# A new order of all pieces in a fused attention and maxout kernel, with w3 loaded first

## The chip, the cores and the metric

The kernel runs on one core of one Trainium2 chip. The metric is the device time of one execution in microseconds (us); lower is better. Engines are called by their names in the profile: PE is TensorE (matrix products; PEld is its weight load), DVE is VectorE, ACT is ScalarE, POOL is GpSimd, SP is SyncE.

## The reference

Eight batches, eight heads, 576 positions, head size 64, 32 memory slots. An attention through 32 slots feeds a maxout layer:

```
a      = softmax(phi, axis = positions)            # 8 x 8 x 576 x 32
k_m    = a^T k ;  v_m = a^T v                      # per head: 32 x 64
attn   = softmax(q k_m^T / 8, axis = slots)        # 576 x 32
x      = attn v_m, heads side by side              # 4608 x 512
h      = max(x w1, x w2, x w3)                     # 4608 x 768
out    = h w_out                                   # 4608 x 512
```

Inputs and output are fp32; the kernel computes in bf16 with fp32 accumulation.

## The kernel before, in words

The kernel does not form x. It multiplies the small v_m into the weights ("fold") and uses attn directly. It also takes w3 out of the maximum: max(x w1, x w2, x w3) is x w3 + max(0, x (w1 - w3), x (w2 - w3)), so the third product needs no maximum and goes through w3 w_out, which is made once (w3T, w3o).

The whole kernel is cut into pieces, and a list at its end (lines 594 to 619) gives their order by hand: a letter, a number and a batch, as F6@1, is one call of `issue`. Each engine takes its instructions in the order in which the list issues them, so the list is the order of every engine at once. An exclamation mark hands the eviction of that piece from ACT to DVE or the other way (`EVAC`, line 164, has the rule without the mark). A string of digits (lines 138 to 146) gives each piece its banks of PSUM, of which there are eight; a piece waits until the eviction of the piece that had its bank is done.

The pieces, with the lines at which the profile shows them:

- L0 to L3: loads of phi, k, v and q of a batch, through POOL's queue (lines 93, 97, 110); phi of batch 0 goes through SP (line 91) ahead of the list. H: a half of k (H0, H2) or v (H1, H3) of batch 0, by pairs of heads. Y0 to Y2: loads of w1, w2, w3 (line 116); Y3: w_out (line 123). All of POOL's loads stand in one queue in the order of the list.
- Z: warm-up matmuls on zeros (line 159), whose results nobody reads. I: the identity and ones, on POOL.
- E: exp(phi) on ACT (line 229). B: a^T k and a^T v, 72 small matmuls (line 249); for batches 0 and 1 B0 does k and B1 does v, for the others B does both, out of a packed copy that r0 and r1 make on POOL (line 103, 2.1 us each). N: the division by the sum on DVE (lines 269, 273, 283). K: the transpose on PE (line 298) and its eviction; K@0 also makes the negative kvtn on ACT (line 304).
- Q0, Q1: transposes of q on DVE (line 313), each waiting for q's load. S: the scores, 32 small matmuls (line 333), then two exps on ACT (line 342).
- For batch 0: M (sums by a matmul, line 354), R (1/sum as exp(-ln) on ACT, lines 366, 372), X (the product on DVE, line 377). For the others: a, s, c on DVE (lines 387, 395, 404), m on POOL (line 409), X on DVE (line 417).
- W, O: w3T and w3o on PE (lines 184, 192), evicted by DVE and by ACT. V: w1 - w3 and w2 - w3 in place, on DVE (line 213). D0 to D2: the folded weights of a batch, 512 columns each (line 440; for batch 0 D0, D1, D2 and D4, with w3 subtracted by further matmuls through kvtn); D3: the folded w3o.
- F0 to F11: the maxout products of a batch, four matmuls each (line 466). Even numbers are w1 - w3, evicted with relu into h (lines 170, 174); odd ones are w2 - w3, whose maximum with h DVE writes to hT (line 479).
- T0 to T4: 128 rows of the output: six matmuls hT by w_out (line 497) and two of attn by the folded w3o (line 506). T4 has 64 rows of each of two batches, so its four matmuls with the folded w3o are narrow, 128 by 64 (line 515). The eviction (line 172 or 176) is followed by the store through SP (line 527). T3@7 is the last piece and goes in two halves (lines 538, 546, 555 to 559).

B, D, S and T4's four use a part of PE's array per matmul ("narrow"); the others use all of it ("wide").

Of the kernel before, what the change touches and what calls it, by code (L numbers as in the profile page):

```python
# [15 lines left out]
def kernel(  # L16
# [18 lines left out]
    NG = NP // 2  # L35
    HP = P // 2
# [4 lines left out]
    FT = DF // P  # L41
# [91 lines left out]
    for i in range(P // M):  # L133
# [14 lines left out]
    def one_bank():  # L148
        return psum[:, int(next(banks))]
# [16 lines left out]
    def evacuate(kind, n, swap, out_, in_, relu=False):  # L166

        if (EVAC[kind][n] == "a") != swap:
            if relu:
                nc.scalar.activation(out=out_, in_=in_, func=AF.Relu)  # L170
            else:
                nc.scalar.copy(out=out_, in_=in_)  # L172
        elif relu:
            nc.vector.tensor_scalar_max(out=out_, in0=in_, scalar1=0.0)
        else:
            nc.vector.tensor_copy(out=out_, in_=in_)
# [245 lines left out]
    wps, wp3s = {}, {}  # L422
# [65 lines left out]
    def ffn2(b, t, swap):  # L488


        hT, attn = hts[b // 2], attns[b // 2]
        c0 = S - HP if t == 4 else (b % 2) * (S + HP) + t * P
        if b == B - 1 and t == 3:
            return ffn2_last(b, c0)
        po = one_bank()
        for n, fc in enumerate(fts[b]):
            nc.tensor.matmul(  # L497
                po,
                lhsT=hT[:, fc, c0 : c0 + P],
                rhs=wo_sb[:, fc, :],  # L500
                start=(n == 0),
                stop=False,
            )
        for g in range(NG):
            if t < 4:
                nc.tensor.matmul(  # L506
                    po,
                    lhsT=attn[:, g, c0 : c0 + P],
                    rhs=wp3s[b][:, g, :],
                    start=False,  # L510
                    stop=(g == NG - 1),
                )
            else:
                for u in range(2):
                    nc.tensor.matmul(  # L515
                        po[HP * u : HP * (u + 1)],
                        lhsT=attn[:, g, c0 + HP * u : c0 + HP * (u + 1)],
                        rhs=wp3s[b - 1 + u][:, g, :],
                        start=False,
                        stop=(g == NG - 1),  # L520
                        tile_position=(0, HP * u),
                    )
        ot = opool.tile([P, DM], FP32, name="ot")
        r0 = (b // 2) * 2 * S + c0
        rows = out[r0 : r0 + P, :]
        evacuate("T", t, swap, ot, po)
        nc.sync.dma_start(out=rows, in_=ot)

    def ffn2_last(b, c0):

        hT, attn = hts[b // 2], attns[b // 2]
        ot = opool.tile([P, DM], FP32, name="ot")
        r0 = (b // 2) * 2 * S + c0
        for i in range(2):
            c = slice(i * DM // 2, (i + 1) * DM // 2)
            po = one_bank()[:, 0 : DM // 2]
            for n, fc in enumerate(fts[b]):
                nc.tensor.matmul(  # L538
                    po,
                    lhsT=hT[:, fc, c0 : c0 + P],  # L540
                    rhs=wo_sb[:, fc, c],
                    start=(n == 0),
                    stop=False,
                )
            for g in range(NG):
                nc.tensor.matmul(  # L546
                    po,
                    lhsT=attn[:, g, c0 : c0 + P],
                    rhs=wp3s[b][:, g, c],
                    start=False,  # L550
                    stop=(g == NG - 1),
                )
# [39 lines left out]


    for w in """
        E@0 L1@0 L3@0 Z25@0 B0@0 I@0 N0@0 Z2@0 K0@0! Q0@0 Q1@0 Z9@0 S@0 Z2@0 M0@0 M1@0
        R0@0 Y2@0 R1@0 W0@0 Y3@0 W1@0 W2@0 Z6@0 O1@0 H3@0 O3@0 O2@0 H1@0 X1@0 B1@0 X0@0 N1@0
        K1@0 O0@0 Y0@0 D1@0! D0@0! D3@0 F8@0 F10@0 F2@0 V0@0 F6@0 F0@0! Y1@0 D2@0 D4@0 F4@0
        L0@1 V1@0 F1@0 E@1 F3@0 L1@1 F5@0 F9@0 F7@0 L3@1 F11@0 B0@1 T3@0 N0@1 K0@1! L2@1 Q1@1
        L2@2 L1@2 Q0@1 L0@2 V2@0 T0@0! L3@2 S@1 T1@0 a0@1 s0@1 c0@1 m0@1 B1@1 N1@1 a1@1 L1@3
        K1@1 s1@1 D0@1 D1@1! D2@1 c1@1 m1@1 X0@1 L3@3 r1@2 X1@1 T2@0! L2@3 F6@1 F10@1 F7@1 F2@1  # L600
        F3@1 F4@1 F0@1 r0@2 E@2 F5@1 F1@1 F11@1 L0@3 L0@4 F8@1 L2@4 F9@1 B@2 D3@1 N@2 Q1@2
        T0@1! K@2 T2@1! r0@3 Q0@2 S@2 a0@2 a1@2 s1@2 c1@2 m1@2 T4@1! D1@2! s0@2 D2@2 c0@2 m0@2
        X1@2 D0@2 T3@1 Q0@3 L3@4 X0@2 Q1@3 T1@1 F0@2 F4@2 F8@2 F6@2 F9@2 E@3 F7@2 r1@3 F5@2
        F10@2 F1@2 B@3 L1@4 D3@2 N@3 L0@5 F2@2 F11@2 E@4 F3@2 L1@5 K@3 r1@4 L2@5 T2@2! S@3 T3@2
        a0@3 s0@3 c0@3 m0@3 D0@3 D2@3 a1@3 s1@3 c1@3 X0@3 D1@3! Q0@4 m1@3 T1@2 L3@5 L2@6 T0@2!
        X1@3 F10@3 r0@4 F2@3 F4@3 E@5 Q1@4 r0@5 F5@3 F3@3 L1@6 F8@3 B@4 N@4 D3@3 F9@3 F6@3
        F11@3 L0@6 K@4 F0@3 F7@3 F1@3 S@4 a0@4 T4@3! s0@4 a1@4 D0@4 c0@4 s1@4 r1@5 c1@4 D3@4
        m0@4 X0@4 Q0@5 T0@3! D1@4! D2@4 B@5 T3@3 m1@4 X1@4 L0@7 F10@4 Q1@5 N@5 F8@4 K@5 F6@4
        F9@4 S@5 F7@4 L3@6 F2@4 F4@4 a0@5 L1@7 a1@5 F0@4 s0@5 r1@6 F3@4 D0@5 r0@6 s1@5 c1@5 E@6
        D3@5 m1@5 c0@5 F1@4 T1@3 L2@7 F11@4 L3@7 E@7 F5@4 m0@5 B@6 D1@5! D2@5 X1@5 N@6 T2@3!  # L610
        X0@5 F6@5 F8@5 Q0@6 Q1@6 K@6 F4@5 F9@5 S@6 F7@5 r0@7 a0@6 F2@5 a1@6 s0@6 c0@6 F0@5
        F10@5 m0@6 F1@5 s1@6 c1@6 F11@5 F5@5 T0@4! F3@5 X0@6 T2@4! r1@7 D0@6 D1@6! Q0@7 B@7
        m1@6 N@7 X1@6 T2@5! K@7 T3@4 Q1@7 S@7 a0@7 F2@6 s0@7 a1@7 s1@7 c1@7 m1@7 c0@7 F4@6
        T4@5! D3@6 D2@7 D0@7! T0@5! D3@7 D2@6 X1@7 m0@7 D1@7! T1@4 X0@7 F6@7 F3@6 T1@5 F4@7
        F8@7 F0@7 F5@6 F10@6 F7@7 F9@7 F10@7 F5@7 F0@6 F11@7 F6@6 F1@7 F7@6 F2@7 F8@6 F11@6
        F9@6 F1@6 F3@7 T0@6! T0@7! T3@5 T2@7! T2@6! T1@6 T1@7 T3@6 T4@7! T3@7
    """.split():
        n, b = w.rstrip("!").split("@")
        issue(int(b), n, w.endswith("!"))
# [30 lines left out]
```

## Time and profile before

| what | value |
|---|---|
| time, median of 3 runs (lowest to highest) | 166.47 us (166.17 to 166.52) |
| span of the profiled execution, first to last instruction | 163.9 us |
| mean granted clock of PE | 1.000 |
| PE busy | 153.8 us (94%), 2080 matmuls |
| DVE, ACT, POOL busy | 90.4, 100.5, 68.8 us |
| DMA moved | 31.77 MB, mean 194 GB/s |
| warm-up matmuls (line 159) | 44, 12.0 us |

The page gives the profiled execution by its span alone; the timed runs hold what lies around the span as well. Matmuls are pipelined: the duration of one (0.38 us for 512 columns) is longer than its distance from the next (0.2155 us), so the distance from start to start is the price of a matmul in a row of them. A bracket in the timeline names the idle time of the engine just before a group and what ended it.

### The profile page before, as it was taken

The numbers are of one execution on the slowest core, as the hardware profiler recorded it, in microseconds if no ns is written. First come the engines' busy times: TensorE is split into PE (matmuls) and PEld (weight loads), VectorE is DVE, ScalarE is ACT, GpSimd is POOL, SyncE is SP. The second block draws the span as 40 slices with busy tenths as digits, with TensorE's granted clock in tenths as the row PEclk, the third lists the DMA queues.
The fourth block names the chain that finished last, engine by engine and source line by source line (L and its number), as shares of the span: only waits on it lengthen the run. The fifth ranks groups of instructions, "written<-read, shape, count | busy, mean of one in ns | idle before, by whom it ended". The sixth has DMA issues, their size and how long they took to land.

```text
span 163.9 us, 4837 instructions
## 1 busy us (share of the span) xinstructions
PE 153.8 (94%) x2080; PEld 85.3 (52%) x2080; DVE 90.4 (55%) x181; ACT 100.5 (61%) x151; POOL 68.8 (42%) x70
## 2 busy tenths in 40 slices
PE   7958798999899999999999999999999999999990
PEld 2423544664376436753673565576553467744450
DVE  2013703898837765759399669879749228810000
ACT  4104535935496488778885989994658976323320
POOL 7911115100698276938929986755403200000000
PEclk9999999999999999999999999999999999999999
DMA  5999999999999999999999999996313230014333
GB/s 149 167 201 207 207 209 226 264 208 209 258 310 239 209 272 361 263 219 294 247 265 206 236 352 254 167 235 148 127 72 119 79 128 0 0 68 179 141 128 130
DMA packets 21958, 31.77 MB, mean 194 GB/s; under 512 B 1200, under 2 KB 16560, under 8 KB 21936
## 3 DMA queue, kind: packets, MB, share of 16 engines
q0 software_dynamic: 16064, 21.43, 68.5%
q1 hardware_dynamic: 5728, 9.90, 17.1%
q8 instruction: 16, 0.26, 0.6%
q10 hardware_dynamic: 144, 0.13, 0.2%
q14 instruction: 6, 0.05, 0.1%
HBM read 39.32 MB, written 9.44 MB: 297 GB/s over the span
## 4 chain that ended last, share of the span: by engine, by line
PE 66%; DMA 27%; POOL 3%; issue 1%; ACT 1%; ACTq 0%; POOLq 0%
PE psum L497 25%; PE psum L466 22%; DMA ph<-in_phi_dram 14%; DMA w_sb<-in_moe_w_dram 12%; PE psum L506 7%; PE psum L440 4%; PE psum L249 3%; PE psum L333 2%; PE psum L515 1%; POOL kvo L97 1%; PE psum L538 1%; ACT e L229 1%; PE psum L298 1%; POOL wo_sb L123 1%; POOL qq L110 0%
## 5 line engine op out<-in xcount | busy, mean ns | idle before, releaser
L497 PE MATMUL psum<-wo_sb,hT 128*128 128x512 bf16 x210 | 51.4, 380 | 0.2
L466 PE MATMUL psum<-attn,wp 128*128 128x288 bf16 x384 | 50.5, 286 | 0.1
L479 DVE TENSOR_TENSOR hT<-psum,h 128x576 bf16<-128x576 f32 x48 | 34.2, 749 | 18.2 <-PE psum L466 12.1
L466 PEld LDWEIGHTS <-wp 128*128 128x128 bf16 x384 | 36.7, 98 | 13.2 <-issue 2.0
L172 ACT COPY ot<-psum 128x512 f32<-128x512 f32 x35 | 20.7, 591 | 32.3 <-PE psum L506 25.2
L497 PEld LDWEIGHTS <-hT 128*128 128x128 bf16 x210 | 19.2, 98 | 24.2 <-issue 4.5
L103 POOL COPY kvr<-kvo 128x2304 bf16<-128x2304 bf16 x12 | 25.4, 2116 | 14.1 <-DMA kvo<-in_k_dram 6.4
L172 ACT CAST wp<-psum 128x1024 bf16<-128x1024 f32 (+1 forms) x31 | 29.3, 997 | 3.0 <-PE psum L440 2.1
L170 ACT ACTIVATE h<-psum 128x576 bf16<-128x576 f32 x47 | 28.4, 659 | 3.2 <-PE psum L466 3.1
L409 POOL TENSOR_TENSOR t<-t,sm 128x576 bf16<-128x576 bf16 x14 | 16.1, 1158 | 25.6 <-DVE sm L404 25.5
L506 PE MATMUL psum<-wp,attn 128*128 128x512 bf16 x62 | 18.4, 379 | 0.0
L159 PE MATMUL psum<-warm 128*128 128x512 bf16 x44 | 12.0, 424 | 1.2 <-DVE warm L128 1.2
L313 DVE STREAM_TRANSPOSE qT<-qq 128x576 f32<-128x576 f32 x16 | 11.7, 747 | 1.3 <-DMA qq<-in_q_dram 1.3
L342 ACT ACTIVATE e<-psum 128x576 bf16<-128x576 f32 x16 | 9.6, 652 | 3.7 <-PE psum L333 3.7
L229 ACT ACTIVATE e<-ph 128x1152 bf16<-128x1152 f32 (+1 forms) x9 | 9.6, 1065 | 2.9 <-DMA ph<-in_phi_dram 2.9
L395 DVE TENSOR_REDUCE sm<-t 128x18 f32<-128x576 bf16 x14 | 10.3, 738 | 0.2
L387 DVE STREAM_TRANSPOSE t<-e 128x288 f32<-128x288 f32 x14 | 6.4, 465 | 6.2 <-ACT e L342 6.0
L506 PEld LDWEIGHTS <-attn 128*128 128x128 bf16 x62 | 6.1, 98 | 7.1
L97 POOL DMA_DIRECT2D kvo<-in_v_dram x9 | 6.7, 747 | 7.1 <-PE psum L249 4.1
L249 PEld LDWEIGHTS <-e 64*32 64x32 bf16 x720 | 6.9, 90 | 4.9 <-issue 3.6
L555 DVE COPY ot<-psum 128x256 f32<-128x256 f32 x1 | 0.4, 425 | 15.4 <-PE psum L546 15.4
L110 POOL DMA_DIRECT2D qq<-in_q_dram x8 | 6.2, 769 | 5.9 <-DMA w_sb<-in_moe_w_dram 5.9
(57 smaller groups left out, 113.8 us busy)
## 6 DMA issues: line engine op xcount, KB each, us to landing
out_dram<-ot SPq DMA_DIRECT2D x35, 256.0 KB, 5.6
kvo<-in_k_dram POOLq DMA_DIRECT2D x8, 576.0 KB, 13.3
qq<-in_q_dram POOLq DMA_DIRECT2D x8, 576.0 KB, 12.6
ph<-in_phi_dram POOLq DMA_DIRECT2D x7, 576.0 KB, 15.0
kvo<-in_v_dram POOLq DMA_DIRECT2D x7, 576.0 KB, 16.6
w_sb<-in_moe_w_dram POOLq DMA_DIRECT2D x3, 768.0 KB, 20.3
wo_sb<-in_moe_w_out_dram POOLq DMA_DIRECT2D x1, 768.0 KB, 15.9
ph<-in_phi_dram SPq DMA_DIRECT2D x2, 288.0 KB, 3.1
```

What stands on the lines that cost most here:

```text
L103: nc.gpsimd.tensor_copy(out=kvrs[b % 2][:, :, :, D * i : D * (i + 1)], in_=kvos[b % 2][:, 1 - i])
L159: nc.tensor.matmul(po[:, 0:BANK], lhsT=warm[:, 0:P], rhs=warm, start=True, stop=True)
L170: nc.scalar.activation(out=out_, in_=in_, func=AF.Relu)
L172: nc.scalar.copy(out=out_, in_=in_)
L229: nc.scalar.activation(out=s["e"][:, js], in_=loaded[b]["ph"][:, js], func=AF.Exp)
L249: nc.tensor.matmul(kvp[M * j : M * (j + 1), a, 0:nd], lhsT=s["e"][r, j, c, :], rhs={None: lambda: kvr[r, j, c, 0:nd], 0: lambda: k_and_one ...
L313: nc.vector.transpose(out=s["qT"][:, j].rearrange("p j c r e -> p (j c r e)").bitcast(FP32), in_=loaded[b]["q"][:, j].rearrange("p j c d - ...
L409: nc.gpsimd.tensor_tensor(out=t, in0=t, in1=s["sm", g].unsqueeze(2).to_broadcast([P, S // HP, R, 2]), op=ALU.mult,)
L466: nc.tensor.matmul(acc[:, h, 0:SH], lhsT=wps[b][:, g, w * DF + ft * P : w * DF + (ft + 1) * P], rhs=attn[:, g, c0 : c0 + SH], start=(g == ...
L479: nc.vector.tensor_tensor(out=hT[:, ft, (b % 2) * S : (b % 2 + 1) * S].rearrange("p (h n) -> p h n", h=2), in0=a, in1=s["h1", ft], op=ALU.max,
L497: nc.tensor.matmul(po, lhsT=hT[:, fc, c0 : c0 + P], rhs=wo_sb[:, fc, :], start=(n == 0), stop=False,)
L506: nc.tensor.matmul(po, lhsT=attn[:, g, c0 : c0 + P], rhs=wp3s[b][:, g, :], start=False, stop=(g == NG - 1),)
```

## The change

Three things. First, the list and the string of banks are replaced as a whole: the pieces are the same, in another order, and other pieces have the exclamation mark. Second, within that, the loads at the start are w3, q, k (in two halves, H2 and H0, in place of one L1), w_out, v, w1, w2 in place of k, q, w3, w_out, v, w1, w2, and the warm-up matmuls are 51, 2 and 2 in place of 25, 2, 9, 2 and 6. Third, T4 does its four narrow matmuls before its six wide ones. The first part of the new list, and the function (the string of banks and the rest of the list are left out):

```diff
@@ ffn2 @@
         po = one_bank()
+        if t == 4:
+            for g in range(NG):
+                for u in range(2):
+                    nc.tensor.matmul(
+                        po[HP * u : HP * (u + 1)],
+                        lhsT=attn[:, g, c0 + HP * u : c0 + HP * (u + 1)],
+                        rhs=wp3s[b - 1 + u][:, g, :],
+                        start=(g == 0),
+                        stop=False,
+                        tile_position=(0, HP * u),
+                    )
         for n, fc in enumerate(fts[b]):
             nc.tensor.matmul(
                 po,
                 lhsT=hT[:, fc, c0 : c0 + P],
                 rhs=wo_sb[:, fc, :],
-                start=(n == 0),
-                stop=False,
+                start=(n == 0 and t < 4),
+                stop=(n == FT - 1 and t == 4),
             )
-        for g in range(NG):
-            if t < 4:
+        if t < 4:
+            for g in range(NG):
                 nc.tensor.matmul(
...
-            else:
-                for u in range(2):
-                    nc.tensor.matmul(
...
@@ the list @@
-        E@0 L1@0 L3@0 Z25@0 B0@0 I@0 N0@0 Z2@0 K0@0! Q0@0 Q1@0 Z9@0 S@0 Z2@0 M0@0 M1@0
-        R0@0 Y2@0 R1@0 W0@0 Y3@0 W1@0 W2@0 Z6@0 O1@0 H3@0 O3@0 O2@0 H1@0 X1@0 B1@0 X0@0 N1@0
-        K1@0 O0@0 Y0@0 D1@0! D0@0! D3@0 F8@0 F10@0 F2@0 V0@0 F6@0 F0@0! Y1@0 D2@0 D4@0 F4@0
-        L0@1 V1@0 F1@0 E@1 F3@0 L1@1 F5@0 F9@0 F7@0 L3@1 F11@0 B0@1 T3@0 N0@1 K0@1! L2@1 Q1@1
-        L2@2 L1@2 Q0@1 L0@2 V2@0 T0@0! L3@2 S@1 T1@0 a0@1 s0@1 c0@1 m0@1 B1@1 N1@1 a1@1 L1@3
-        K1@1 s1@1 D0@1 D1@1! D2@1 c1@1 m1@1 X0@1 L3@3 r1@2 X1@1 T2@0! L2@3 F6@1 F10@1 F7@1 F2@1
-        F3@1 F4@1 F0@1 r0@2 E@2 F5@1 F1@1 F11@1 L0@3 L0@4 F8@1 L2@4 F9@1 B@2 D3@1 N@2 Q1@2
-        T0@1! K@2 T2@1! r0@3 Q0@2 S@2 a0@2 a1@2 s1@2 c1@2 m1@2 T4@1! D1@2! s0@2 D2@2 c0@2 m0@2
-        X1@2 D0@2 T3@1 Q0@3 L3@4 X0@2 Q1@3 T1@1 F0@2 F4@2 F8@2 F6@2 F9@2 E@3 F7@2 r1@3 F5@2
...
+        Y2@0 L3@0 E@0 I@0 H2@0 Q0@0 H0@0 Y3@0 Z51@0 B0@0 Q1@0 N0@0 W0@0 H1@0 Z2@0 K0@0 H3@0
+        Y0@0 W1@0 Y1@0 S@0 W2@0 L0@1 M0@0 O0@0 L1@1 M1@0 R1@0 L3@1 L2@1 O3@0 B1@0 N1@0 R0@0
+        O2@0 X0@0 L1@2 K1@0 O1@0 D1@0 D0@0 X1@0 D3@0 Z2@0 F10@0! F6@0 F2@0 V0@0 F0@0 D2@0! D4@0
+        F8@0 V1@0 F3@0 F7@0 F9@0 F1@0 E@1 L2@2 F4@0 L0@2 F5@0 B0@1 F11@0 N0@1 T1@0 L3@2 K0@1
+        T3@0 Q1@1 Q0@1 L1@3 S@1 B1@1 V2@0 N1@1 a0@1 s0@1 a1@1 c0@1 s1@1 c1@1 m0@1 m1@1 r0@2
+        L2@3 r1@2 K1@1! L0@3 L3@3 L2@4 X0@1 r0@3 T0@0 D0@1 X1@1 L1@4 D2@1 D1@1 T2@0! F2@1 F6@1
+        F0@1! F8@1 F1@1 F10@1 E@2 F9@1 F11@1 F4@1 F3@1 F5@1 F7@1 D3@1 B@2 N@2 L0@4 Q1@2 r1@3
+        T3@1! K@2! Q0@2 T1@1 S@2 a0@2 s0@2 c0@2 a1@2 s1@2 m0@2 c1@2 m1@2 L3@4 L2@5 L1@5 r1@4
+        T0@1 D0@2 r0@4 D3@2! D1@2 E@3 T4@1! X0@2 T2@1! X1@2 D2@2 B@3 N@3 Q1@3 F10@2 Q0@3 F2@2
...
```

More of the change, by code (lines that the diff above doesn't have):

```diff
@@ L140 @@
             """
-            00224460026701101401264026402640264026452063420643064206420642064562074206742064
-            20642064201640264102640264026402640264072406247026402640264024602406520462046204
-            62704267402640264124602416420642064206420642067676767670
+            60263024120414012042604624064026402645246001642046042640624062452463640234062460
+            24062046024206520406402460426016241246104062562046046204620426402462064026074202
+            460236204704264207604604602640624026402042604654545456
             """.split()
@@ L512, in ffn2 @@
                 )
-            else:
-                for u in range(2):
[L515 to L522, printed above, removed]
         ot = opool.tile([P, DM], FP32, name="ot")
@@ L601 @@
-        F3@1 F4@1 F0@1 r0@2 E@2 F5@1 F1@1 F11@1 L0@3 L0@4 F8@1 L2@4 F9@1 B@2 D3@1 N@2 Q1@2
-        T0@1! K@2 T2@1! r0@3 Q0@2 S@2 a0@2 a1@2 s1@2 c1@2 m1@2 T4@1! D1@2! s0@2 D2@2 c0@2 m0@2
-        X1@2 D0@2 T3@1 Q0@3 L3@4 X0@2 Q1@3 T1@1 F0@2 F4@2 F8@2 F6@2 F9@2 E@3 F7@2 r1@3 F5@2
-        F10@2 F1@2 B@3 L1@4 D3@2 N@3 L0@5 F2@2 F11@2 E@4 F3@2 L1@5 K@3 r1@4 L2@5 T2@2! S@3 T3@2
-        a0@3 s0@3 c0@3 m0@3 D0@3 D2@3 a1@3 s1@3 c1@3 X0@3 D1@3! Q0@4 m1@3 T1@2 L3@5 L2@6 T0@2!
-        X1@3 F10@3 r0@4 F2@3 F4@3 E@5 Q1@4 r0@5 F5@3 F3@3 L1@6 F8@3 B@4 N@4 D3@3 F9@3 F6@3
@@ L607 @@
[L607 to L616, printed above, removed]
+        Y2@0 L3@0 E@0 I@0 H2@0 Q0@0 H0@0 Y3@0 Z51@0 B0@0 Q1@0 N0@0 W0@0 H1@0 Z2@0 K0@0 H3@0
+        Y0@0 W1@0 Y1@0 S@0 W2@0 L0@1 M0@0 O0@0 L1@1 M1@0 R1@0 L3@1 L2@1 O3@0 B1@0 N1@0 R0@0
@@ new lines @@
+        T0@1 D0@2 r0@4 D3@2! D1@2 E@3 T4@1! X0@2 T2@1! X1@2 D2@2 B@3 N@3 Q1@3 F10@2 Q0@3 F2@2
+        F4@2 F3@2 F0@2 F11@2 F5@2 F6@2 F1@2 F7@2 K@3! F8@2 F9@2 S@3 E@4 T1@2 a0@3 s0@3 D3@3
+        c0@3 D2@3! L0@5 D1@3! a1@3 T0@2! B@4 D0@3 T3@2 s1@3 m0@3 c1@3 X0@3 Q0@4 m1@3 L3@5 X1@3
+        Q1@4 F6@3 N@4 F2@3! F8@3 r1@5 F4@3 F9@3 F0@3 F10@3! L0@6 F7@3 F1@3 F3@3 r0@5 F5@3 K@4
+        T2@2! F11@3 L1@7 L2@6 E@5 S@4 T3@3! D1@4! B@5 a0@4 Q1@5 N@5 s0@4 c0@4 L1@6 D2@4 T4@3!
+        K@5 a1@4 m0@4 T1@3 Q0@5 L3@6 s1@4 c1@4 S@5 D0@4 X0@4 a0@5 a1@5 s0@5 m1@4 T2@3! X1@4
@@ new lines @@
+        c0@5 D1@5 D0@5 D2@5 L0@7 s1@5 c1@5 T0@3! L2@7 F8@4 F2@4 m0@5 m1@5 F4@4 X1@5 F10@4 X0@5
+        F9@4 F3@4 r1@6 L3@7 r0@6 E@6 F0@4 F5@4 F10@5 F6@5! F8@5 F1@4 F11@4 F6@4 F7@4 F2@5 F11@5
+        F4@5 r0@7 F9@5 F0@5 F3@5 B@6 Q1@6 Q0@6 r1@7 D3@4 D3@5 N@6 T1@4 F1@5 K@6! F7@5 E@7 F5@5
+        T3@4! Q0@7 S@6 a0@6 B@7 N@7 D1@6 T0@4 Q1@7 s0@6 K@7! T3@5! D0@6 a1@6 S@7 T4@5! a0@7
+        c0@6 s1@6 D2@7 m0@6 a1@7 c1@6 D0@7! m1@6 D3@6 T2@4 s1@7 D1@7 D2@6 D3@7 T1@5 X0@6 X1@6
+        T2@5! F2@6 s0@7 c1@7 F4@6! m1@7 c0@7 X1@7 F5@6 T0@5! m0@7 X0@7 F8@6! F10@6 F6@6! F3@6
@@ L617 @@
+        F0@6 F6@7 F11@6 F1@6 F2@7 F9@6 F8@7 F7@6 F10@7! F3@7 F0@7 T1@6! F7@7 F4@7! F11@7 F5@7
+        F1@7 T2@6! F9@7 T3@6 T2@7! T4@7 T1@7! T0@7! T0@6 T3@7
     """.split():
```

## The prediction

> **What bounds the kernel now.** I read the table of busy time by stretches first, then the start-up and the gaps of TensorE in the timeline, then the chain that ended last for the price of each piece.
>
> The stretches (columns: length, then busy us and instruction count of PE, PEld, DVE, ACT and POOL, granted clock, DMA share, GB/s):
>
> ```profile
> 10.00:16.00 6.00, 5.17 (x122) 2.33 (x122) 2.22 (x5) 1.63 (x4) 1.50 (x2) 1.00 1.18 207
> 24.00:28.00 4.00, 3.57 (x121) 1.76 (x119) 0.72 (x3) 1.90 (x4) 2.09 (x3) 1.00 1.17 213
> 40.00:44.00 4.00, 3.25 (x105) 1.59 (x105) 3.17 (x8) 1.93 (x5) 1.57 (x2) 1.00 1.19 239
> 60.00:80.00 20.00, 20.00 (x259) 11.11 (x244) 13.86 (x29) 16.66 (x25) 14.23 (x14) 1.00 1.14 286
> 120.00:140.00 20.00, 20.00 (x198) 11.54 (x197) 11.04 (x19) 14.75 (x23) 2.27 (x2) 1.00 0.21 80
> ```
>
> TensorE has next to no gap from 28 us to its end at 160.2. A new order can win there only the few waits that are left, and it can lose by making new ones. Before 28 us TensorE is filled up with warm-up matmuls and waits for loads; the DMA engines are busy throughout (share above 1) and move some 210 GB/s.
>
> Which loads, the timeline's start-up and gaps show (start, duration, instruction, in brackets the idle time before it and what ended it):
>
> ```profile
> 1.19 7.21 PE L159 MATMUL psum<-warm 128*128 128x512 bf16 x25 [1.19 <-DVE warm L128]
> 9.94 0.80 PE L249 MATMUL psum<-kvo,e 64*32 64x128 bf16 x72 [1.54 <-DMA kvo<-in_k_dram]
> 16.47 1.34 PEld L184 LDWEIGHTS <-w_sb 128*128 128x128 bf16 x24 [0.39 <-DMA w_sb<-in_moe_w_dram]
> 20.25 4.04 PE L192 MATMUL psum<-wo_sb,w3T 128*128 128x512 bf16 x18 [0.97 <-DMA wo_sb<-in_moe_w_out_dram]
> 30.65 0.11 PEld L440 LDWEIGHTS <-kvt 64*32 64x32 bf16 x8 [0.24 <-DMA w_sb<-in_moe_w_dram]
> 52.39 0.81 PE L249 MATMUL psum<-kvr,e 64*32 64x129 bf16 x72 [0.37 <-ACT e L229]
> ```
>
> The loads stand in one queue and land in order. Issue time plus time to landing gives k 9.8, q 12.7, w3 16.5, w_out 20.2, v 23.1, w1 26.8, w2 30.6, then for batch 1 phi 32.2, k 34.8, q 37.7, v 40.5, and phi of batch 2 51.2. D1@0 starts at 26.9, on w1's landing, and D2@0 at 30.65, on w2's. The two landings are the clock of the start-up; what TensorE has not done by then comes on top.
>
> The chain that ended last, in order of time, prices the pieces (start, us, what):
>
> ```profile
> 58.97 0.55 PE psum L515 x4
> 59.52 0.77 PE psum L440 x24
> 60.30 1.40 PE psum L497 x6
> 61.70 0.43 PE psum L506 x2
> 62.13 1.29 PE psum L497 x6
> 63.42 0.43 PE psum L506 x2
> 63.86 4.41 PE psum L466 x36
> ```
>
> An F is 4.41/9 = 0.49, a T 1.29 + 0.43 = 1.72. The six wide matmuls take 1.40 behind narrow ones (D, B, S, T4's) and 1.29 behind wide ones: 0.11 for leaving a narrow shape, and entering one costs about 0.1 too (narrow ones of T4: 0.55 against two pairs at 2 x 0.215). Likewise from this chain and the timeline: D 0.22, B 0.59 to 0.76, S 0.42, O 1.29, W 0.45.
>
> **The change part by part.**
>
> *T4, narrow matmuls first.* Four pieces, the same ten matmuls; one entry and one exit of the narrow shape either way. Cost 0. Bounds: four entries of 0.12 saved or added, 0.5 both ways. The time goes by the count below.
>
> *The order on TensorE.* Counting each piece at its price, with 0.1 for each change of shape, the work from D1@0 to the last matmul is 130.4 us before and 130.7 after, of which 0.43 is a Z2 (two warm-up matmuls) newly behind D3@0; without it the new order is 0.13 cheaper, since it goes into narrow shapes three times less in the whole kernel. From D2@0 to the first F of batch 1 (F6@1 before, F2@1 after) it is 14.18 and 14.58: F8@0 now stands behind D2@0. From that F to the end it is 112.9 in both.
>
> *Loads.* w3, q and both halves of k are together the 1,920 KB that k, q and w3 were; they land by 16.5. So k of batch 0 lands at 16.5 and not at 9.8, half 0 last, and B0 reads half 0 first, so the halves give nothing. w_out, v, w1 and w2 keep their places and times. There is one DMA more on POOL's queue; in the trace the ninth waits for the first to land (POOL idles 2.03 for k at 10.09), so w2's issue would wait for w3 at about 11, 19 us ahead of its landing: hidden. make_identity and the memsets (1 us on POOL) move ahead of k's issue, hidden behind w3's and q's 6 us of data.
>
> *Warm-up.* 51 matmuls instead of 25 at first: 26 x 0.2155 more, end 13.8. TensorE then idles to 16.5, 2.7 us, where the longest gap before was 1.54.
>
> *The start-up after 16.5*, walked with the durations of before's rows. All of B0, W, S, M, B1, K1 and the four O now lies behind 16.5: 9.9 us of TensorE with the Z2. B0 to 17.25; N0 on DVE as before, so K0 at 16.5 + 1.73 = 18.2; its eviction now stands on DVE behind W0's (0.63), kvt at 19.1; S to 19.6, first exp to 20.3, M0; O0 from 20.6, M1, O3 to 23.6, B1 (v 23.1 is there), O2, K1, O1 to 27.1. D1@0 at 27.15 against 26.89: w1 is waited for no longer, TensorE itself is late by 0.26. X0 (DVE, behind R0's Ln and Exp on ACT to 25.9) ends 26.7, kvtn 27.3, D1's eviction 28.25, X1 28.95: F10's second half starts 29.05. F6, F2, F0 to 30.8, **D2@0 at 30.9: +0.25**.
>
> *Evictions behind D2@0.* ACT does O1's, D0 (1.0), D3 (1.0), F6, F2, F0 (0.65 each) without pause from 28.1 to 32.1, then D4 to 33.1. F7 needs D4's columns and could start at 32.6: wait 0.5 (before D4's eviction ended 2.0 us behind D2@0's start, now 2.2 and one F less lies ahead of it). On DVE V0, D2, V1 end at 33.4, then the six max at 0.75: B0@1 waits 0.2 more. Q0@1 (q 37.7, DVE busy until K0's eviction at 39.4) ends 40.95, S@1 waits 0.15. V2 (1.18) now stands on DVE ahead of N1@1: N1 ends 42.55, K1@1 waits 0.55 for it where B1@1 ended. X1@1 ends 47.35, F2@1's second half waits 0.25. With 0.15 of small ones these waits are 1.8; the same stretch of before holds 15.32 - 14.18 = 1.14. So the first F of batch 1 starts at 30.9 + 14.58 + 1.8 = 47.3 against 45.98: **+1.33** = 0.25 + 0.40 + 0.68. Bounds of the waits: below, none more than before (0); above, each eviction one further 0.75 late on DVE at the two places where two of them queue (+1.5).
>
> *From there to the end.* Before holds 114.23 - 112.93 = 1.30 of waits. The largest is B@2 for phi of batch 2 (0.43: landing 51.2, exp 1.17). phi 2 lands at the same time after, only k and v of batch 2 change places, and B@2 is not due before 47.3 + 6.2 = 53.5: **-0.43**. The other 0.87 I leave as they are; bounds: all gone (-0.87) or as many again (+0.87).
>
> Sum: 1.33 - 0.43 = +0.90. The page gives the profiled execution only by its span, 163.9; it becomes 164.8. The median of the timed runs, 166.47, lies 2.5 above the span, for what is around it; nothing there changes (last store, same last piece). Time 166.47 + 0.90 = 167.4.
>
> **The rivals.**
>
> *The start-up keeps up (other side).* If k lands 1 us earlier (w3's 1,536-byte packets moved 208 GB/s where k's 1,152-byte ones moved 160 to 190 in the first microseconds), D1@0 waits for w1 again and ACT gets D4 done in time. Then 0.25 and 0.68 fall away: 0.40 - 0.43, 166.4; and if the order also drops the small waits, 165.6. It decides from k before about 15.7. Against it: the landing of before already has that slow phase in it, and V2 and N1 stay on DVE in that order whatever lands. Chance 0.24.
>
> *Batch 3 late on POOL and DMA.* r1@3 (2.1 on POOL, waits for v of batch 3) now stands ahead of m0@2 and m1@2 (1.15 each); v 3 lands about 60.7 in the place that q 3 had, so m1@2 ends 65.1, X1@2 65.6, and F10@2 is due at 65.65. No room: 1 us later landing is 1 us of TensorE. phi 3 (about 63) with its exp leaves B@3 at 64.9 about as little. +0.5 to +1.3: 168.2 on average. Chance 0.16.
>
> *The clock falls in the 2.7 us gap.* The first warm-ups stand 0.43 apart until 4.6 us and 0.2155 after; after the 1.54 gap B0 still took 0.80 as later ones did (0.81). No row shows a 2.7 us gap. If the slow pace came back for the 3.4 us that it lasted at first, half of that, 1.7, is added to the 9.9 us behind 16.5: 169.1. Chance 0.08. [...]
>
> **How the numbers follow.** Forecast 167.4, chance 0.52; rivals 0.24, 0.16, 0.08. About 0.2% (0.33 us) is what a measurement can tell. The forecast's own spread reaches below 166.8 with 0.06; the first rival splits into 0.17 faster and 0.07 same. So faster 0.17, same 0.13, slower 0.70. The range 166.0 to 168.8 takes in the forecast with its bounds, the batch-3 rival and half of the first; it leaves out the clock and the lower half of the first, about 0.18.
>
> **What would show it.** B0@0 starts at 16.5 after a gap of 2.7 on k; D1@0 waits for TensorE's own work, not for w1; D2@0 at 30.9; F7@0 waits for ACT's wp; K1@1 for N1; F2@1 at 47.3; no wait before B@2. I am wrong if D2@0 starts on w2's landing and F2@1 before 46.4, or if F10@2 or B@3 waits for POOL or phi.

## The result and the profile after

The new order is slower: 167.42 us (median of 18 runs, 166.44 to 168.18) against 166.24 (18 runs, 164.92 to 166.79). The ratio is 1.0072, with a 95% interval of 1.0052 to 1.0093: 1.2 us lost, by the interval 0.86 to 1.55. The forecast was 167.4.

The profiled execution of the new order has a span of 165.8 us, 1.9 above the 163.9 of before. In every execution for which both are listed, the time is 1.7 to 1.9 above the span. So the profiled execution of before took about 165.7, itself 0.5 under its median, and the one of after took 167.56, 0.1 above its own. Two profiles alone would overstate the loss by 0.7 us.

The page of after, PE's granted clock and the engines:

```profile
span 165.8 us, 4862 instructions
PE 156.3 (94%) x2091; PEld 87.8 (53%) x2091; DVE 111.1 (67%) x207; ACT 85.1 (51%) x125; POOL 69.5 (42%) x71
PEclk9999699999999999999999999999999999999998
```

PE has 11 matmuls more (the warm-ups, 55 for 44). The exclamation marks moved evictions from ACT (100.5 busy before, 85.1 now) to DVE (90.4, now 111.1); both still have room. There is one dip of the clock, at about 18 us. The profiled execution of after is the only one of its 18 with a granted clock below 0.995, so what it shows of the start-up is not the usual case; the experiments below show that.

The table of stretches of after, with the columns of the one before:

```profile
10.00:16.00 6.00, 3.78 (x18) 1.51 (x16) 1.44 (x2) 0.00 (x0) 1.95 (x3) 1.00 1.21 206
16.00:22.00 6.00, 4.99 (x134) 3.62 (x135) 2.77 (x7) 0.87 (x2) 1.77 (x3) 0.72 1.22 207
24.00:28.00 4.00, 4.00 (x89) 2.05 (x88) 1.09 (x3) 3.69 (x7) 0.84 (x2) 1.00 1.16 210
40.00:44.00 4.00, 3.57 (x117) 1.80 (x115) 3.73 (x7) 2.50 (x5) 0.00 (x0) 1.00 1.21 209
60.00:80.00 20.00, 19.12 (x333) 10.39 (x332) 18.47 (x34) 14.10 (x21) 15.29 (x14) 1.00 1.17 252
120.00:140.00 20.00, 20.00 (x194) 10.40 (x193) 16.67 (x31) 11.09 (x16) 4.60 (x4) 1.00 0.27 99
```

From 10 to 16 us PE has only warm-ups left (3.78 busy, 18 matmuls for 122 before). The moved work now stands behind 16 us (134 matmuls from 16 to 22), and from 24 to 28 PE is full (4.00 for 3.57). From 60 to 80 it has a hole of 0.88 that was not there.

The timeline of after at the places that the prediction named:

```profile
16.83 0.80 PE L249 MATMUL psum<-kvo,e 64*32 64x128 bf16 x72 [3.05 <-DMA kvo<-in_k_dram]
28.43 0.13 PEld L440 LDWEIGHTS <-kvt 64*32 64x32 bf16 x8 [0.42 <-DVE kvt L176]
32.21 0.11 PEld L440 LDWEIGHTS <-kvt 64*32 64x32 bf16 x8 [0.24 <-issue]
34.19 2.32 PEld L466 LDWEIGHTS <-wp 128*128 128x128 bf16 x20 [0.32 <-ACT wp L172]
43.33 0.23 PE L298 MATMUL psum<-ident,kvn 128*128 128x128 bf16 x1 [0.43 <-DVE kvn L273]
47.73 4.45 PE L466 MATMUL psum<-attn,wp 128*128 128x288 bf16 x35
```

These are B0@0 behind its gap, D1@0, D2@0, the F that waits for ACT's D4, K1@1 behind N1, and F2@1, the first F of batch 1. In this execution D1@0 follows O1@0 on PE, 0.55 after w1 landed (27.88; landings are worked out as in the prediction, issue plus time to landing). The bracket names kvt, but DVE had evicted that by 28.10, and PEld idles 0.42 in that place in before as well.

Where the difference between two executions arises, by marks on PE (us). The loads run ahead or behind from one execution to the next, so the fairest pair is before and the first experiment, *e1* below, which differs from the changed kernel in 13 warm-up matmuls alone: by 30 us the two had moved 5.42 and 5.43 MB through POOL's queue (all other profiles 5.20 to 5.28), and both had the full clock. Even so w2 landed 0.68 later in e1 (31.25 for 30.57).

| | before | after | e1 | e1 − before | forecast |
|---|---|---|---|---|---|
| D2@0 starts | 30.65 | 32.21 | 31.29 | +0.64 | +0.25 |
| from there to the first F of batch 1 | 15.33 | 15.52 | 15.99 | +0.66 | +0.40 + 0.68 |
| from there to the last matmul | 114.23 | 114.32 | 113.98 | −0.25 | −0.43 |
| sum | – | – | – | +1.05 | +0.90 |

By these marks the loss of e1 lies ahead of 48 us, as forecast, but with other sizes. The marks alone do not say what sets the end: behind 48 us the new order waits for a load in every profile but two, and e8 below shows how much hangs on that.

### The profile page after: what moved, and what is told of

Same layout as the page of the kernel before. It is cut to its first block, busy times and chain, and to the rows that moved or that the text cites. A ratio compares the mean times of both kernels' runs of the same rounds, so it can differ in the third digit from the quotient of the medians.

```text
span 165.8 us, 4862 instructions
## 1 busy us (share of the span) xinstructions
PE 156.3 (94%) x2091; PEld 87.8 (53%) x2091; DVE 111.1 (67%) x207; ACT 85.1 (51%) x125; POOL 69.5 (42%) x71
## 4 chain that ended last, share of the span: by engine, by line
PE 85%; DMA 7%; POOL 2%; ACT 2%; issue 1%; DVE 1%; ACTq 0%; POOLq 0%
PE psum L466 29%; PE psum L509 28%; PE psum L518 8%; DMA kvo<-in_k_dram 7%; PE psum L440 6%; PE psum L249 4%; PE psum L192 3%; PE psum L333 2%; PE psum L500 1%; PE psum L184 1%; PE psum L298 1%; PE psum L159 1%; PE psum L540 1%; DVE wp L176 1%; ACT wp L172 1%
## 5 line engine op out<-in xcount | busy, mean ns | idle before, releaser
L466 PE MATMUL psum<-attn,wp 128*128 128x288 bf16 x384 | 49.9, 286 | 0.1
L172 ACT COPY ot<-psum 128x512 f32<-128x512 f32 x23 | 13.5, 586 | 30.2 <-PE psum L518 27.8
L170 ACT ACTIVATE h<-psum 128x576 bf16<-128x576 f32 x38 | 23.7, 651 | 9.1 <-PE psum L466 8.2
L172 ACT CAST wp<-psum 128x1024 bf16<-128x1024 f32 x23 | 22.6, 1018 | 7.7 <-PE psum L440 7.6
L176 DVE COPY ot<-psum 128x512 f32<-128x512 f32 x12 | 8.2, 681 | 12.3 <-PE psum L518 7.6
L159 PE MATMUL psum<-warm 128*128 128x512 bf16 x55 | 14.2, 419 | 1.2 <-DVE warm L128 1.2
L176 DVE CAST wp<-psum 128x1024 bf16<-128x1024 f32 (+1 forms) x10 | 10.9, 1097 | 1.1 <-PE psum L440 0.9
L174 DVE TENSOR_SCALAR h<-psum 128x576 bf16<-128x576 f32 x10 | 7.6, 756 | 4.0 <-PE psum L466 4.0
L159 PEld LDWEIGHTS <-warm 128*128 128x128 bf16 x55 | 5.6, 106 | 8.2 <-issue 2.1
L97 POOL DMA_DIRECT2D kvo<-in_k_dram x9 | 6.7, 739 | 7.7 <-PE psum L249 4.9
```

The lines of the kernel that those rows point to most:

```text
L159: nc.tensor.matmul(po[:, 0:BANK], lhsT=warm[:, 0:P], rhs=warm, start=True, stop=True)
L466: nc.tensor.matmul(acc[:, h, 0:SH], lhsT=wps[b][:, g, w * DF + ft * P : w * DF + (ft + 1) * P], rhs=attn[:, g, c0 : c0 + SH], start=(g == ...
```

## The experiments

All were timed in five rounds. Ratios are against the kernel before on the same chip, with 95% intervals.

**e1_z64: the gap closed.** 13 more warm-up matmuls ahead of B0@0.

```diff
-Y3@0 Z51@0 B0@0
+Y3@0 Z64@0 B0@0
```

> The changed kernel with 64 warm-up matmuls first in place of 51, which end at about 16.4 and close the gap ahead of B0@0 (nothing else differs). Clock theory (the half-clock window from 17.7 to 21.1 in the changed kernel's profile comes from the 3.05 us gap and costs time to the end): granted clock 1.000 to the end, D2@0 at 30.9 instead of 32.2, and a time 0.4 to 1.3 below the changed kernel, 166.1 to 167.0. Backlog theory (the clock only moves waits about; what counts is that k lands last and TensorE's work of the start-up lies behind it): D2@0 earlier, but the first F of batch 1 still at 47.3 and 167.0 to 167.4.

**e2_z40: the gap widened.**

```diff
-Y3@0 Z51@0 B0@0
+Y3@0 Z40@0 B0@0
```

> The changed kernel with 40 warm-up matmuls first in place of 51: the gap ahead of B0@0 grows from 3.05 to about 5.4 us, so that a window of half clock follows in every execution. Clock theory: if only some executions of the changed kernel have the half clock, this one is slower in the median, 167.7 to 168.2, with less spread; D2@0 at 32.2 or later. Backlog theory: no more than 0.2 beside the changed kernel, 167.2 to 167.6.

Measured: e1 166.89, ratio 1.0072 [1.0043, 1.0102]; e2 167.34, ratio 1.0068 [1.0032, 1.0105]. (e1's time lies in the range given for the clock theory, but before was 166.04 beside it; the ratio, the same as the changed kernel's, speaks against that theory.) All 12 listed executions of e1 have a granted clock of 0.995 or more, all 9 of e2 one of 0.977 to 0.990. The stretch from 16 to 22 us, first of e1, then of e2 (the clock is the third figure from the end):

```profile
16.00:22.00 6.00, 5.70 (x145) 3.47 (x144) 2.96 (x7) 1.20 (x3) 1.48 (x2) 1.00 1.22 206
```

```profile
16.00:22.00 6.00, 5.22 (x136) 3.84 (x137) 3.14 (x7) 1.19 (x2) 1.50 (x3) 0.72 1.23 208
```

And from the timelines, the first F of batch 1 in e1 and B0@0 in e2:

```profile
47.28 2.00 PE L466 MATMUL psum<-attn,wp 128*128 128x288 bf16 x15
```

```profile
16.54 1.16 PE L249 MATMUL psum<-kvo,e 64*32 64x128 bf16 x72 [4.21 <-DMA kvo<-in_k_dram]
```

The clock is 1.00 in e1 and 0.72 in e2, and B0@0 takes 1.16 for 0.80. Yet the first F of batch 1 stands at 47.30 in e2 and at 47.28 in e1. In part that is chance: e1 lost 0.41 to a w2 that landed 0.68 later than e2's, and 0.32 where PE stops in the middle of B1@1 and no engine or load is named. e2's median is 0.45 above e1's; the two intervals overlap, so neither a cost of that size nor none is excluded. In the profiles the two differ behind that F (114.74 and 113.98 to the last matmul), at one place: B@4, which e8 below explains. The dip in the profile of after isn't the cause of the loss: e1, and 17 of the 18 executions of after, lose as much without it.

**e3_oldstart: the start-up of before up to D3@0, then the new order from F10@0.**

```diff
-Y2@0 L3@0 E@0 I@0 H2@0 Q0@0 H0@0 Y3@0 Z51@0 B0@0
...
-O1@0 D1@0 D0@0 X1@0 D3@0 Z2@0 F10@0!
+E@0 L1@0 L3@0 Z25@0 B0@0 I@0 N0@0 Z2@0 K0@0!
...
+K1@0 O0@0 Y0@0 D1@0! D0@0! D3@0 Y1@0 L0@1 L1@1 L3@1 L2@1 L1@2 Z2@0 F10@0!
```

> The start-up of the kernel before (its order, loads and warm-ups up to D3@0, k whole and first) and from F10@0 on the new order, with the new T4. Start-up theory (all of the loss is made before the first F of batch 1): D2@0 at 30.7, F2@1 at 46.0 to 46.4, time 166.0 to 166.5. Rest theory (the new order behind the start-up loses through waits such as the 0.86 ahead of B@4): 166.8 to 167.4, with that wait still there or larger.

**e4_newstart: the new start-up up to D3@0, then the order of before from F8@0.**

```diff
-K1@0 O0@0 Y0@0 D1@0! D0@0! D3@0 F8@0 F10@0
+K1@0 O1@0 D1@0 D0@0 X1@0 D3@0 F8@0 F10@0
```

> The new start-up up to D3@0 (w3 first, k in halves, 51 warm-ups, one Z2 behind D3@0) and from F8@0 on the order of the kernel before, with the new T4. Start-up theory: D2@0 at 31 to 32.2, first F of batch 1 (F6@1) 0.8 to 1.5 later than before's 45.98, the wait ahead of B@2 gone or smaller, time 166.9 to 167.6. Rest theory: 166.0 to 166.5.

Measured: e3 167.46, ratio 1.0084 [1.0055, 1.0112]; e4 168.61, ratio 1.0152 [1.0097, 1.0207]. e3 is just above its rest theory, e4 above both of its theories. Neither is a clean half: at the seam the banks of the two lists do not fit. In e3 PE idled 1.04 us ahead of the Z2 behind D3@0, until DVE had evicted a D ahead of the seam; in e4 the first two F came about 1.3 late. So they tell nothing of the parts.

**e5_oldstart2: e3 without the Z2, and the banks of the second half renamed** so that it takes up those that are free at the seam (the digits 0 and 1 of the string became 2 and 3, 2 and 3 became 4 and 5, 4 and 5 became 6 and 7, 6 and 7 became 0 and 1).

```diff
-L1@2 Z2@0 F10@0!
+L1@2 F10@0!
-00224460026701101401264604624064026402645246...
+00224460026701101401264260462062406240674602...
```

> As the first old-start kernel (start-up of the kernel before up to D3@0, then the new order from F10@0), with two faults of that one mended: the banks of the new part are renamed so that no piece right behind the seam takes the bank of a piece right ahead of it (there Z2 waited 1.12 us for D3@0's eviction), and that Z2 is left out. Start-up theory: D2@0 at 30.7 to 31.0, F2@1 at 46.2 to 46.6, 0.6 to 1.0 below the changed kernel: 166.3 to 166.8. Rest theory (from F10@0 on the new order loses by itself, whatever lies ahead): F2@1 at 46.8 to 47.3, 167.0 to 167.4.

**e6_newstart2: e4 with the Z2 behind D3@0 and the banks renamed the other way.**

```diff
-X1@0 D3@0 F8@0
+X1@0 D3@0 Z2@0 F8@0
```

> As the first new-start kernel (new start-up up to D3@0 and its Z2, then the order before from F8@0), with the banks of the old part renamed so that nothing waits at the seam (there F8@0 and F10@0 lost 1.3 us). Start-up theory: F6@1 at 46.6 to 47.2, time 0.5 to 1.0 above before, 166.7 to 167.2. Rest theory: F6@1 at 46.0 to 46.3, time within 0.3 of before, 166.0 to 166.4.

Measured: e5 167.38, ratio 1.008 [1.005, 1.0111]; e6 167.58, ratio 1.0087 [1.0052, 1.0121]. Each half alone loses as much as the whole, so the two halves don't add up: e5 came out as its rest theory, e6 above both of its own. In e5's profile B0@1 waits for k of batch 1:

```profile
36.56 0.80 PE L249 MATMUL psum<-kvo,e 64*32 64x128 bf16 x72 [1.10 <-DMA kvo<-in_k_dram]
```

In e6's profile, an execution 1.0 above e6's median, B@2 waits for POOL's second copy of batch 2; POOL had begun the first when v of batch 2 landed, at 50.09. Phi of that batch had landed at 51.63, and its exp was done at 53.3:

```profile
55.10 0.80 PE L249 MATMUL psum<-kvr,e 64*32 64x129 bf16 x72 [1.12 <-POOL kvr L103]
```

A split at D3@0 can't say what the start-up costs by itself: an order that is early at one place meets a load at the next.

**e7_t4: the kernel before, with T4's narrow matmuls first and nothing else.** The edit is the first hunk of the diff of the change.

> The kernel before with T4's narrow matmuls first, and nothing else. By the prediction's count (one entry and one exit of the narrow shape either way) within 0.1 of before: 165.9 to 166.4, and each T4 with the piece ahead of it within 0.05 us of before. Rival: narrow ones first let TensorE run while the last hT is still evicted, or the exit ahead of the wide ones costs more: 0.1 per T4, 0.4 in all, either way.

Measured: 166.69, ratio 1.0025 [0.9998, 1.0051]: not told from no change, and no gain. By the trace T4@5 takes 2.54 with what stands ahead of it where it took 2.43; it is now entered from a wide piece and left into a narrow one. T4@1 takes 2.376 in both, T4@7 3.681 for 3.670. T4@3 can't be compared: PE stops in it in both profiles, for 0.3 in before and for 0.6 here, with no engine or load named. This profile is of an execution 0.8 above e7's median, and it holds something else, with a start-up that is before's to the letter:

```profile
36.81 0.80 PE L249 MATMUL psum<-kvo,e 64*32 64x128 bf16 x72 [1.35 <-DMA kvo<-in_k_dram]
```

In the profile of before the k of batch 1 landed at 34.8 and nothing waited. The same load in the same place landed 1.9 us later here, at 36.7.

**e8_phi4: phi of batch 4 loaded earlier.** In the changed kernel, both loads right behind E@2, phi first.

```diff
-X1@1 L1@4 D2@1
+X1@1 D2@1
-E@2 F9@1
+E@2 L0@4 L1@4 F9@1
-N@2 L0@4 Q1@2
+N@2 Q1@2
```

> The changed kernel with the load of phi of batch 4 issued ahead of k of batch 4, both right behind E@2, in place of the other way round. In the changed kernel's profile E@4 holds ACT until phi 4 lands at 75.6, D3@3's eviction stands behind it on ACT, and B@4 waits 0.86 us for D3@3's banks. If that wait is of the end time: phi 4 lands at about 72, the wait goes, and the time falls by 0.5 to 0.9, to 166.6 to 166.9. Rival: k of batch 4, now later by phi's 1.7 us, holds r0@4 and B@4 instead, or the wait comes back at a later batch: within 0.3 of the changed kernel, 167.1 to 167.6.

Measured: 166.96, ratio 1.0045 [1.0024, 1.0065], between the two forecasts. Behind the hole between 60 and 80 us stands this in the changed kernel:

```profile
75.63 1.16 ACT L229 ACTIVATE e<-ph 128x1152 bf16<-128x1152 f32 x1 [1.35 <-DMA ph<-in_phi_dram]
77.17 1.93 ACT L172 CAST wp<-psum 128x1024 bf16<-128x1024 f32 x2
78.23 0.80 PE L249 MATMUL psum<-kvr,e 64*32 64x129 bf16 x72 [0.78 <-ACT wp L172]
```

E@4, the exp of phi, holds ACT until phi has landed; the evictions of D are queued behind it; B@4 on PE waits for their banks. The name in B@4's bracket is that of the eviction, but the cause stands one row up, in ACT's own bracket: a DMA. In e8 the chain is gone:

```profile
73.19 1.17 ACT L229 ACTIVATE e<-ph 128x1152 bf16<-128x1152 f32 x1
74.68 2.11 POOL L103 COPY kvr<-kvo 128x2304 bf16<-128x2304 bf16 x1 [2.49 <-DMA kvo<-in_k_dram]
76.84 0.80 PE L249 MATMUL psum<-kvr,e 64*32 64x129 bf16 x72 [0.37 <-POOL kvr L103]
80.36 1.88 PE L466 MATMUL psum<-attn,wp 128*128 128x288 bf16 x14 [0.41 <-DVE attn L417]
```

E@4 waits for nothing, but k of batch 4 went behind phi, so POOL's copy of it is late, B@4 still waits 0.37, and 0.41 come back at the next F. From the first F of batch 1 to the end e8 took 114.47 us, after 114.32: the wait has moved more than gone. The ratio is the lowest of all kernels with the whole new order, yet its interval overlaps the changed kernel's.

The wait for phi of batch 4 (phi 4) weighs more than the marks in the section on the result show. In e1 it is the same chain as in after:

```profile
74.83 1.16 ACT L229 ACTIVATE e<-ph 128x1152 bf16<-128x1152 f32 x1 [1.00 <-DMA ph<-in_phi_dram]
77.43 0.80 PE L249 MATMUL psum<-kvr,e 64*32 64x129 bf16 x72 [0.44 <-ACT wp L172]
```

All profiles with the new order from F10@0 on (us; e10 and e11 follow below):

| | first F of batch 1 | phi 4 lands | B@4 starts | last matmul ends |
|---|---|---|---|---|
| after | 47.73 | 75.61 | 78.23 | 162.05 |
| e1 | 47.28 | 74.81 | 77.43 | 161.25 |
| e2 | 47.30 | 75.61 | 78.23 | 162.04 |
| e3 (start-up of before) | 47.18 | 75.04 | 77.66 | 161.49 |
| e5 (start-up of before) | 47.53 | 75.41 | 78.04 | 161.86 |
| e9 (k whole) | 47.54 | 75.43 | 78.05 | 161.86 |
| e8 (phi 4 earlier) | 46.76 | 71.87 | 76.84 | 161.23 |
| e10 (F8@0 earlier) | 48.61 | 75.49 | 78.26 | 162.07 |
| e11 (e10 and e8) | 48.77 | 71.29 | 78.42 | 162.23 |

In the first six rows B@4 starts 2.62 or 2.63 behind phi 4's landing, and the last matmul ends 83.8 behind B@4, whatever the start-up, the gap and the clock were. In e10 and e11 PE comes to B@4 late enough to wait for nothing, and the stretch from the first F to the end takes 113.46; in the first six it takes 0.5 to 1.3 more, and that is the wait. So in these profiles the end hangs on the landing of one load: a start-up slower by up to that wait would not have ended later, and a quicker one ends sooner only if phi 4 lands sooner too. That is why e5, with the start-up of before, ends where the changed kernel does, and why e1 and e2 differ at B@4 alone: phi 4 landed 0.80 later in e2. What the new order would take with the start-up in time and no wait at B@4 no run shows; in e8 k of batch 4 took phi's place.

**e9_kwhole: k of batch 0 in one load again, in the changed kernel.**

```diff
-H2@0 Q0@0 H0@0 Y3@0
+L1@0 Q0@0 Y3@0
```

> The changed kernel with k of batch 0 loaded whole (one L1@0 in the place of H2@0; H0@0 left out). The prediction counts the halves at nothing: k lands at 16.2 to 16.8, B0@0 starts then, w2 is issued 3 us earlier but lands no earlier, time within 0.3 of the changed kernel, 167.1 to 167.7. Rival: with one load less on POOL's queue w2 is issued at 8 in place of 11 and lands 0.4 earlier, so D2@0 and the end come 0.4 earlier: 166.8 to 167.1.

Measured: 167.28, ratio 1.0067 [1.0046, 1.0088], and B0@0 starts at 16.75 (16.83 in after). No gain or cost of the halves can be told. (B0@1 waited 0.96 for k of batch 1 here too.)

**e10_f8: e1, with F8@0 ahead of D2@0 again and F1@0 behind F3@0** (and the banks of four pieces of batch 0 changed to fit).

```diff
-F0@0 D2@0! D4@0 F8@0 V1@0 F3@0 F7@0 F9@0 F1@0
+F0@0 F8@0 D2@0! D4@0 V1@0 F3@0 F1@0 F7@0 F9@0
```

> The changed kernel with 64 warm-ups first (as in the first experiment) and F8@0 again ahead of D2@0, as in the kernel before (and F1@0 behind F3@0, so that F7, which needs D4's columns, comes later; banks of F8, F1, F7 and D4 of batch 0 changed to fit). If the piece that stands behind w2's landing in the new order costs what the prediction says: D2@0 still at w2's landing, F2@1 0.4 earlier against it (D2@0 to F2@1 15.1 in place of 15.5 to 16.0), time 0.3 to 0.5 below the 64 warm-ups alone, ratio to before 1.004 to 1.006. Rival (F2@1 hangs on the loads of batch 1 and on ACT and DVE, not on that piece): within 0.2 of it, ratio 1.006 to 1.008.

**e11_f8phi4: the edits of e10 and of e8 together** (the 64 warm-ups of e1 included; the two loads leave their old places as in e8).

```diff
-F0@0 D2@0! D4@0 F8@0 V1@0 F3@0 F7@0 F9@0 F1@0
+F0@0 F8@0 D2@0! D4@0 V1@0 F3@0 F1@0 F7@0 F9@0
...
-E@2 F9@1
+E@2 L0@4 L1@4 F9@1
```

> The former kernel (64 warm-ups, F8@0 ahead of D2@0) with phi of batch 4 loaded ahead of k of batch 4 as well. If the two gains add: ratio to before 1.000 to 1.003, 166.0 to 166.6. Rival (they do not add; what is won is waited for at the next load): ratio 1.004 to 1.006.

Measured: e10 167.85, ratio 1.0104 [1.0086, 1.0123]; e11 167.72, ratio 1.0107 [1.0079, 1.0134]: slower than the changed kernel by their medians, and above both forecasts of each. The F that was put ahead of the wait for w2 filled that wait; but what it freed was lost at once, in e10:

```profile
33.34 3.18 PE L466 MATMUL psum<-attn,wp 128*128 128x288 bf16 x24 [0.46 <-DVE wp L176]
37.20 0.80 PE L249 MATMUL psum<-kvo,e 64*32 64x128 bf16 x72 [0.68 <-DVE hT L479]
```

F3 now comes as soon as D2's columns are due from DVE, which evicts them from 32.59 to 33.28, and B0@1 then waits for a bank that DVE empties late. F8@0 behind D2@0 was cover for that eviction. The first F of batch 1 comes at 48.61, later than in any kernel above, and this time PE's own lateness sets the end (table above).

**e12_z32: the kernel before with 32 instead of 25 first warm-ups**, so that its gap on k is closed.

```diff
-L3@0 Z25@0 B0@0
+L3@0 Z32@0 B0@0
```

> The kernel before with 32 warm-up matmuls first in place of 25; they end at 9.75, about when k lands. In 11 of 24 executions of the kernel before the mean granted clock was 0.985 to 0.990, that is one window of half clock, and their median was 0.6 above that of the others. If that window comes from the gap between the warm-ups and B0@0: clock 0.995 and more in every execution, and the median falls by 0.2 to 0.4, ratio 0.997 to 0.999. Rival: the window has another cause, or the late loads make both the gap and the long time: ratio 0.999 to 1.001.

Measured: 167.01, ratio 1.0051 [1.0032, 1.0071]: slower, which neither forecast had, with a clock of 0.995 or more in 8 of 8. B0@0 starts at 10.44 (9.94 before) and the first F of batch 1 at 46.48, 0.50 later than in before's profile, which was a quick execution. What is left lies far behind, where PE stops in the middle of a piece, in S@4:

```profile
86.42 0.47 PE L333 MATMUL psum<-qT,kvt 32*32 32x288 bf16 x29
87.97 0.30 PE L333 MATMUL psum<-qT,kvt 32*32 32x288 bf16 x3 [1.08 <-issue]
```

29 of its 32 matmuls run, then PE idles for 1.08 and no engine or load is named. From 85.61 us on, for 0.95 us, a packet of 16,384 bytes of the queue of instructions was moving. Before has a stop of 0.3 one piece later, at 88.02, behind a packet from 85.64 to 86.61; the changed kernel has none there.

No version that was run is faster than the kernel before.

## Why the prediction was right, and where it was not

*The sum.* Forecast +0.90, measured +1.18 [0.86, 1.55]: sign and size were right. In good part that was luck, for wrong terms made up for each other. The waits ahead of the first F of batch 1, +0.68, did not grow; w2, which was to keep its time, was late in e1 by chance; and a wait that was put at nothing, for phi 4, came behind that F.

*The base.* "The median lies 2.5 above the span, for what is around it" was wrong in its reason: about 1.8 is around the span, and the rest is that the profiled execution was shorter than most. The forecast added its terms to the median, so the number did not suffer.

*T4 at nothing.* The interval of e7, −0.03 to +0.85 us (0.9998 and 1.0051 times 166.31, less that), holds the forecast; the traces show 0.12 in the three pieces that can be compared. Its upper part stays open.

*Loads and the halves.* Right: k was put at 16.5, B0@0 started between 16.2 and 17.4 in the nine profiles with the new start-up, and in e9 no effect of the halves can be told. The gap was 3.05 in the profile, for 2.7.

*The start-up, +0.25 for PE's own backlog.* As a delay of its own it shows where the clock was halved: in after D1@0 and D2@0 start 0.55 and 0.52 behind the landings of w1 and w2, and no load is waited for. At full clock "w1 is waited for no longer" did not hold. In e1, e8, e9, e10 and e11 D1@0 starts 0.13 or 0.14 behind w1's landing each time, and in e8 and e11 PE visibly waits for it; this is e8:

```profile
27.47 0.30 PE L440 MATMUL psum<-w_sb,kvt 64*32 64x256 bf16 x8 [0.38 <-DMA w_sb<-in_moe_w_dram]
```

D2@0 starts on w2, 0.04 to 0.14 behind its landing, in e1, e8, e9 and e10; this is e1:

```profile
31.29 0.30 PE L440 MATMUL psum<-w_sb,kvt 64*32 64x256 bf16 x8 [0.41 <-DMA w_sb<-in_moe_w_dram]
```

PE itself was ready there at 30.88, 0.23 after before's start, which is the forecast; the other 0.41 of the +0.64 is w2, at 31.25 for 30.57. The new order of loads does not by itself make w2 late: e2, which has it too, had w2 at 30.57, and e3, with before's order, at 31.46.

*F8@0 behind D2@0, +0.40.* Right as a count. e10 shows that it can't be had back by moving F8@0 alone.

*The waits up to the first F of batch 1, +0.68.* This step failed. From D2@0 to that F, after, e2, e3 and e8 all took 15.52, 0.19 more than before's 15.33. F8@0 is 0.40 of that, so the waits fell by 0.21. (e1's 15.99 holds the stop in B1@1, 0.32, that no engine or load explains.) F7 did wait for ACT's D4, for 0.2 to 0.3 and not 0.5. K1@1 did wait for N1, but in before it waits as long:

```profile
42.92 0.23 PE L298 MATMUL psum<-ident,kvn 128*128 128x128 bf16 x1 [0.43 <-DVE kvn L273]
```

Nor is V2 on DVE the reason in the new order:

```profile
42.98 0.29 DVE L273 TENSOR_TENSOR kvn<-psum,rden 128x128 bf16<-128x128 f32 x1 [0.20 <-PE psum L249]
```

V2 was done at 42.78; N1 itself waited 0.20 for B1's matmuls, and K1, right behind B1, waits for N1 whatever stands on DVE. And before's wait of 0.32 for kvt ahead of D0@1 is gone.

*From there to the end, −0.43.* The wait for phi of batch 2 went, as said: no idle time stands ahead of B@2. But "the other 0.87 I leave as they are" failed. Without a wait at B@4 the new order takes 113.46 there (e10, e11), 0.77 less than before's 114.23; the wait for phi 4 adds 0.86 to that in after and 0.5 in e1, so the stretch comes to +0.09 and −0.25. This term was put at nothing, and by the table under e8 it is where the end of the new order is set in the profiles.

*The rivals.* At full clock the start-up did keep up with the loads, as the first rival has it, but its gain did not come: the first F of batch 1 stood at 46.76 at the earliest (e8), and the end waited for phi 4. So of the prediction's signs of being wrong, D2@0 on w2's landing came and F2@1 before 46.4 did not. Batch 3 was not late on POOL: F10@2 didn't wait. The mechanism came one batch later and through another engine, phi of batch 4 through ACT. The clock did fall in the profile of after, in 1 of its 18 executions: it was 0.50 from 17.72 to 21.13, for 3.41 us, where the rival had put 3.4. The rival's chance was an estimate, and its price of 1.7 was too high: e2, with a clock of 0.977 to 0.990 in all 9 listed executions, has a median 0.45 above e1's, with intervals that overlap.

*Still open.* Why the new start-up with the old rest (e6) loses the whole loss, and why e12, with a fuller start-up, loses 0.5%. What moves the landings is not known either. In the profiles a load that lands up to 1.9 us later, or a stop of PE beside the instruction queue (1.08 in e12), takes back what the order gives. The latter is an argument from coincidence: in e7 an instruction packet moved from 34.58 to 35.53, just ahead of the late k of batch 1, but in before one moved from 34.09 to 34.98 and the same load was on time; and no run took these packets away.

## What to carry to other kernels

In a stream that is full, price an order by its waits one by one: here the wait that went at one place (phi of batch 2, 0.37) came back at another (phi of batch 4), and there an exp that waited 1.35 for its load held back the evictions behind it on ACT, and PE idled 0.78 for their banks. Look for the last load that PE waits for: in six profiles the last matmul ended 83.8 behind B@4, which stood 2.62 or 2.63 behind that load's landing, and what was won ahead of it did not reach the end; in e10 and e11 PE came later than that, and what it had lost did. A piece that stands behind a matmul whose eviction is awaited may be its cover: F8@0 stood behind D2@0, and with F8@0 ahead of it, in e10, PE waited 0.46 for that eviction. Compare two profiles only once their loads have been compared; here the landing of one load moved by 1.9, more than the whole effect of 1.2. A forecast that comes out can still be right by luck; only its terms, measured one by one, show that.

## What was unexpected of the hardware

Half clock came also behind gaps shorter than the 2.7 us that the prediction's rival spoke of. In e5 the 3.41 us ahead of the stretch at half clock held 1.40 us of PE's work, in after, with the gap of 3.05, 0.89 (columns as in the stretches; these are e5's two):

```profile
7.45:10.86 3.41, 1.40 (x76) 0.79 (x73) 0.00 (x0) 0.00 (x0) 1.16 (x2) 1.00 1.17 192
10.86:14.27 3.41, 3.41 (x22) 1.12 (x11) 2.14 (x5) 0.37 (x1) 0.95 (x2) 0.50 1.18 214
```

PE's longest gap in the first of them was 2.01 us; in e7 a gap of 1.90 was followed by half clock too (from 11.54 to 14.96; mean 0.63 from 12 to 16), while in e4 one of 2.54 was not (clock 1.000). So in these profiles the length of the gap alone does not decide, and no run shows what does. The kernel before, whose longest gap in its profile is 1.54, had a clock of 0.990 or less in 21 of 66 executions beside the experiments. Their median is 166.22, that of the other 45 is 166.05; the difference is +0.6 in the first of the three groups of executions and −0.1 and +0.15 in the others, so no steady cost shows.

The loads' progress is another matter of chance: by 10 us the profiled executions had moved between 0.92 and 1.10 MB through POOL's queue, and what waits for a load later shifts with it.
